# Attention scores of the two smallest query chunks in plain float32, with one head in each of two opposite quarters of the array

## The chip, the cores and the metric

The kernel runs on one core of a Trainium2 chip. The metric is the device time of the whole program in microseconds (us), as the median of several runs. The core has a tensor engine (PE, with its weight loads shown as PEld), VectorE (DVE), ScalarE (ACT), GpSimd (POOL) and SyncE (SP), whose queue issues nearly all of the DMAs here.

## What is computed

Three layers follow one another: causal attention with a bias from a cumulative sum, a dense feed-forward layer, and a layer of eight experts of which each token takes one. Only the first is touched. Cut to what matters:

```python
# q, k, v: (4, 8, 576, 64) float32; s: (4, 8, 576)
scores = (1 / sqrt(64)) * (q @ k.T)
cum = cumsum(maximum(s, 0), axis=-1)
bias = -(cum[:, :, :, None] - cum[:, :, None, :])
scores = where(causal, -1e9, scores + minimum(bias, 0))
attn = exp(scores - scores.max(-1))
attn = attn / (attn.sum(-1) + 1e-9)
x = attn @ v                                  # then to (2304, 512)
x = (h - tanh(h)) @ w_out,  h = x @ w_in
out = expert layer of x, one expert for a token
```

## The kernel before

The attention works on 16 pairs of heads (4 batches with 4 pairs each). `attention_events` makes the work of one pair as a list of events, each with a time in schedule steps; a pair starts every 9 steps, and all events of all pairs are sorted by these times. On PE the instructions stand in exactly this order (`manual_schedule` with `ORD[MA]`, which holds PE alone); on the other engines and on SP's queue a scheduler orders them by its own model, with the time of the event as priority.

For each pair the 576 queries are cut into nine chunks of 64 (`NCH`). Chunk c sees the first 64c + 64 keys. A chunk's scores for both heads stand in one PSUM tile `sc`: head 0 in partitions 0 to 63, head 1 in 64 to 127. They come from one matmul over all 128 rows: the queries stand in `qb` as blocks (rows 0 to 63 and columns 0 to 63 for head 0, rows 64 to 127 and columns 64 to 127 for head 1, zeros between), the keys of both heads one under the other. To keep precision, queries and keys are split in a rounded high part and the rest (`qh`, `ql`, `kh`, `kl`, type float32r), and three products are added (L235 and L236). The split is made per pair by ACT (L192, L200: the high parts) and by POOL (L183, in `low`: the rests; for the first pair by DVE).

The chunks are scored from the largest (c = 8, step 0 of the pair) to the smallest (c = 0, step 8). Chunks 2 and 0 share the PSUM tile of chunks 3 and 1 (`SECOND`): chunk 1 fills columns 0 to 127, chunk 0 columns 128 to 191, and then one mask matmul in bfloat16 adds the causal mask for both (L243). For the other chunks the mask is a matmul of its own (L246). DVE adds the bias and takes the row minimum (L254), ACT takes the exponential (L258). PE then transposes the weights in groups of four blocks of 128 by 128 (`ptr`, L273), DVE and ACT copy them to `PT` (L137), and PE multiplies them with the values (`pv`, L292), plain float32, head 0 into partitions 0 to 63 and head 1 into 64 to 127. On PE one group of transposes stands before chunk 1, one between chunk 1 and chunk 0, and one behind chunk 0's mask.

The denominators `den` are transposed (L318), written to memory (`rden_d`, L325), read back spread over partitions (`rdb`, L343) and multiplied in when `pv` is evacuated (L300). The biases of the scores come from POOL (L211), from rows `cr` that are loaded for each pair (L178). Queries and keys are loaded by L160 as [128, 576] tiles `xq` and `xk`, two buffers each. `pads` (events at step 60.5) clears some records on POOL (L415 to L419) and sends them out through SP (L417, L420). For the last pair the denominators are spread by small plain float32 matmuls instead (L336), written as a loop over chunks and the two heads:

```python
nc.tensor.matmul(
    pt[64 * h:64 * h + 64, 64 * c - o:64 * c - o + 64], k.oh[:, c, :], T["rt"][:, 64 * h:64 * h + 64],
    start=True, stop=True)
```

While the attention runs, ACT and DVE also convert weights of the next layer (L402 to L406). The next layer begins on PE with L597.

Of the kernel before, what the change touches and what calls it, by code (L numbers as in the profile page):

```python
# [8 lines left out]
F32 = mybir.dt.float32  # L9
# [29 lines left out]
def setup_attention(ctx, tc, k, s):  # L39
# [58 lines left out]
    for p in k.P:  # L98
# [10 lines left out]
SECOND = (2, 0)  # L109
# [4 lines left out]
BIAS = 'PPPPPPPPP'  # L114
LO = 'PPP'

AT = {'ni': 14, 'no': 2, 'pad': 60.5, 'const': 42.5, 'wl': 6.2, 'cr': -9.0, 'load': -20.0, 'v': 6.0, 'ks': -9.5, 'qs': -8.5,
# [11 lines left out]
def behind(tc, k, eng, ins):  # L129

    if eng in k.mark:
        tc.add_manual_dep(
            ins.ins, k.mark[eng], mybir.DependencyInfo(mybir.DependencyClass.NoSync, mybir.DependencyReason.DATA), reason="queued behind")
# [6 lines left out]
def attention_events(tc, k, q, kk, v, xT, b, hp, idx):  # L140

    nc = tc.nc
# [3 lines left out]
    T = {}  # L146
    P = k.P[idx % 2]
    qh, ql = k.qb[idx % NQB]

    def at(t):  # L150
        def deco(f):
            ev.append((9 * idx + t, f))
            return f
        return deco

    @at(AT["load"])
    def _():
        for src, nm in ((kk, "xk"), (q, "xq")):
            t = T[nm] = k.e1.tile([128, S], F32, name=nm, tag=nm, bufs=2)
            nc.sync.dma_start(t, src[b, hp])  # L160

    @at(AT["v"])
    def _():
        t = T["vt"] = ld.tile([128, 2, 5, D], F32, name="vt", tag="vt", bufs=2)
        nc.sync.dma_start(t.rearrange("p a c d -> p (a c d)"), v[b, hp])

    @at(AT["cr"] if idx else AT["qs"] + 0.1)
    def _():
# [12 lines left out]
    def low(eng, l, x, h):  # L181
        pool = idx and eng == "P"
        ins = (nc.gpsimd if pool else nc.vector).tensor_tensor(l, x, h.bitcast(F32), ALU.subtract)  # L183
        if pool:
            behind(tc, k, "P", ins)
            k.mark["P"] = ins.ins.name

    @at(AT["ks"])
    def _():
# [4 lines left out]

    @at(AT["qs"])
    def _():
        for h in range(2):
            p, o = slice(64 * h, 64 * h + 64), slice(64 * h, 64 * h + 64)
            x = T["xq"][p].rearrange("p (c i) -> p c i", i=64)
            behind(tc, k, "A", nc.scalar.copy(qh[p, :, o], x))  # L200
            low(LO[1 + h], ql[p, :, o], x, qh[p, :, o])

    def chunk(c, lo=0, hi=None):
        return P[:, PW[c] + lo:PW[c] + (64 * c + 64 if hi is None else hi)]
# [1 line left out]
    def bias(c):  # L206

        w = 64 * c + 64
        ci = k.cumi[:, c, bh // 2:bh // 2 + 1]
        if BIAS[c] == "P" and (idx or c % 2):  # L210
            ins = nc.gpsimd.tensor_scalar(chunk(c), T["cr"][:, 0:w], 1.0, ci, ALU.mult, ALU.add)  # L211
            behind(tc, k, "P", ins)
            k.mark["P"] = ins.ins.name
        else:
            nc.vector.tensor_scalar(chunk(c), T["cr"][:, 0:w], ci, None, ALU.add)


    def score(c):
        if c == NCH - 1:
            T["m"] = wk.tile([128, NCH], F32, name="m", tag="m")  # L220
            T["m2"] = wk.tile([128, 1], F32, name="m2", tag="m2")
            T["den"] = wk.tile([128, NCH], F32, name="den", tag="den")
        w = 64 * c + 64

        if w > 512:
            cuts = [(0, 288, 0), (288, 576, 0)]
        else:
            cuts = [(0, w, 64 * c + 128 if c in SECOND else 0)]
        for lo, hi, o in cuts:
            two = c in SECOND or c - 1 in SECOND  # L230
            if c not in SECOND:
                T["sc"] = ps.tile([128, 512], F32, name="sc", tag="sc")
            sc, n = T["sc"], hi - lo

            for i, (a, x) in enumerate(((qh, "kh"), (qh, "kl"), (ql, "kh"))):  # L235
                nc.tensor.matmul(  # L236
                    sc[:, o:o + n], a[:, c, :], T[x][:, lo:hi], start=(i == 0 and c not in SECOND), stop=(i == 2 and hi < w))
            if c - 1 in SECOND:
                continue
            if c in SECOND:  # L240

                d = sc[:, o - 64:o + n].rearrange("p (a j) -> p a j", j=64)
                nc.tensor.matmul(  # L243
                    d[:, 0::c + 1, :], k.identb, k.maskm.unsqueeze(1).broadcast_to((128, 2, 64)), start=False, stop=True)
            elif hi == w:
                nc.tensor.matmul(sc[:, n - 64:n], k.identb, k.maskm, start=False, stop=True)  # L246
            if c in SECOND:
                least(c + 1, sc, 0, 0, w + 64, 3.0e38)
            least(c, sc, o, lo, hi, 3.0e38 if lo == 0 else T["m2"])

    def least(c, sc, o, lo, hi, start):
        dst = chunk(c, lo, hi)
        m = T["m"][:, c:c + 1] if hi == 64 * c + 64 else T["m2"]
        k.mark["D"] = nc.vector.tensor_tensor_reduce(  # L254
            out=dst, in0=sc[:, o:o + hi - lo], in1=dst, scale=-0.125, scalar=start, op0=ALU.add, op1=ALU.min, accum_out=m).ins.name
# [5 lines left out]
    for n in range(NCH):  # L261
        at(n + AT["bias"] - (4 if idx == 0 and n % 2 else 0))(lambda c=NCH - 1 - n: bias(c))
        at(n)(lambda c=NCH - 1 - n: score(c))
        at(n + AT["exp"] + (0.6 if NCH - 2 - n in SECOND else 0))(lambda c=NCH - 1 - n: expo(c))
# [734 lines left out]
def tile_kernel(ctx, tc, q, kk, v, s, w_in, w_out, w_gate, w_og, w1, w2, out, dbg=None):  # L999
# [7 lines left out]
    with ExitStack() as abctx:  # L1007
# [3 lines left out]
        with ExitStack() as actx:  # L1011
# [14 lines left out]
            for i in range(16):  # L1026
                ev += attention_events(tc, k, q, kk, v, xT, i // 4, i % 4, i)
# [81 lines left out]
```

## Time and profile before

| | us |
|---|---|
| median of 3 runs | 928.68 (928.37 to 930.35) |
| the profiled execution | 928.81 |
| its span in the profile | 927.1 |
| attention, from the start to the first L597 matmul on PE | 197.5 |
| busy over the span: PE, DVE, ACT, POOL | 884.7 (95%), 613.5 (66%), 537.9 (58%), 367.4 (40%) |

The profile lists for each instruction its start and duration on the profiled execution. The ends of matmuls are modelled, and matmuls overlap in the array, so a matmul's price is read from start to start and not from its duration. A row of the timeline merges instructions of the same line and form that follow one another: its first number is the start of the first, its second the time from there to the end of the last, and "x4" their count; with the duration of a single one the start of the last is found. In brackets stand the idle time of the engine before the row and what ended it. The same line can be called "L292 pv<-PT,vt": it writes `pv` and reads `PT` and `vt`; "128*64" are the array's rows and columns that it uses.

### The profile page before, as it was taken

Reading aid. Unit: us, or ns where it says so; the run is one execution under the profiler, and the core shown is the slowest. Engines: PE = TensorE matmul, PEld = TensorE weight load, DVE = VectorE, ACT = ScalarE, POOL = GpSimd, SP = SyncE. Lnnn points to the kernel's source line nnn. Section 1 sums busy time; section 2 is a strip of 40 time slices with the busy share of each in tenths; the row PEclk is TensorE's granted clock in tenths of the full one; section 3 lists DMA queues with packets and bytes.
Section 4 is the critical chain, followed back from the end, with each engine's and each line's share of the span. In section 5 each row is a group of like instructions: output and inputs, shape, how many; then the busy total and the mean of one; then the engine's idle time right before and its main releaser. Section 6 shows DMA issues by size and latency. Waiting matters only on the chain.

```text
span 927.1 us, 16181 instructions
## 1 busy us (share of the span) xinstructions
PE 884.7 (95%) x5808; PEld 757.2 (82%) x5809; DVE 613.5 (66%) x1343; ACT 537.9 (58%) x1092; POOL 367.4 (40%) x396
## 2 busy tenths in 40 slices
PE   7999999988998999999999999999799999999995
PEld 5777787777877778888989898988688888888884
DVE  8988988969888887786565656577435444444420
ACT  6887888856666667465555555565254444444421
POOL 8999788725444432342222232322230220221011
PEclk9999999999999999999999999999999999999998
DMA  6676776562212211000000000422655554565100
GB/s 210 202 209 191 228 211 185 191 234 69 58 57 69 69 46 69 1 24 2 24 1 24 2 23 1 124 105 91 151 209 169 164 179 152 167 191 145 49 25 30
DMA packets 41362, 100.82 MB, mean 109 GB/s; under 512 B 9314, under 2 KB 9446, under 8 KB 41278
## 3 DMA queue, kind: packets, MB, share of 16 engines
q1 hardware_dynamic: 37117, 89.51, 31.4%
q0 software_dynamic: 4160, 10.23, 3.2%
q8 instruction: 47, 0.77, 0.4%
q14 instruction: 38, 0.30, 0.1%
HBM read 84.74 MB, written 15.79 MB: 108 GB/s over the span
## 4 chain that ended last, share of the span: by engine, by line
PE 62%; DVE 14%; issue 9%; ACT 5%; POOL 4%; DMA 4%; SPq 1%; DVEq 0%; POOLq 0%; ACTq 0%
PE h L597 14%; PE x L627 12%; PE y L864 12%; PE hc L840 10%; PE sc L236 4%; PE pv L292 3%; DVE d L609 3%; PE tp L273 3%; DVE t L611 3%; POOL P L211 2%; DVE d L607 2%; DVE wt L405 1%; DVE wt L406 1%; DMA rdb<-rden_d 1%; ACT u L604 1%
## 5 line engine op out<-in xcount | busy, mean ns | idle before, releaser
L597 PE MATMUL h<-x_h,wi 128*128 128x256 f32 x1152 | 221.4, 285 | 3.3 <-DVE t L610 3.3
L614 POOL TENSOR_TENSOR gl<-t,gh 128x512 fp32r<-128x512 f32 x72 | 100.4, 1395 | 259.8 <-ACT gh L613 173.0
L597 PEld LDWEIGHTS h<-x_h,wi 128*128 128x128 f32 x1152 | 184.0, 191 | 11.2 <-PE x L627 6.4
L627 PE MATMUL x<-wo,gh 128*128 128x512 f32 x576 | 180.0, 393 | 0.3 <-POOL wo L545 0.3
L597 PE MATMUL h<-x_l,wi 128*128 128x256 f32 x576 | 162.8, 283 | 0.0
L627 PE MATMUL x<-wo,gl 128*128 128x512 f32 x288 | 114.8, 399 | 8.4 <-POOL gl L614 8.3
L607 DVE TENSOR_TENSOR d<-u,h 128x512 f32<-128x512 f32 x72 | 49.4, 686 | 105.5 <-ACT t L606 105.4
L627 PEld LDWEIGHTS x<-wo,gh 128*128 128x128 f32 x576 | 103.6, 189 | 18.6 <-POOL wo L545 0.7
L597 PEld LDWEIGHTS h<-x_l,wi 128*128 128x128 f32 x576 | 110.2, 191 | 1.3
L236 PE MATMUL sc<-kh,qb 128*128 128x288 f32 (+8 forms) x320 | 100.7, 344 | 0.0
L258 ACT ACTIVATE P<-P,m 128x576 f32<-128x576 f32 (+2 forms) x144 | 81.1, 566 | 22.7 <-DVE m L254 22.1
L613 ACT CAST gh<-t 128x512 fp32r<-128x512 f32 x72 | 44.7, 621 | 83.3 <-DVE t L611 59.8
L827 DVE SCALAR_TENSOR_TENSOR gl<-hc,gh 128x336 fp32r<-128x336 f32 (+2 forms) x66 | 32.8, 497 | 90.5 <-ACT gh L826 84.0
L211 POOL TENSOR_SCALAR P<-cr,cumi 128x448 f32<-128x448 f32 (+4 forms) x139 | 88.1, 650 | 1.9 <-ACT cr L137 0.4
L826 ACT ACTIVATE gh<-hc 128x336 fp32r<-128x336 f32 (+2 forms) x66 | 29.2, 443 | 94.9 <-PE hc L840 83.2
L840 PE MATMUL hc<-xgh,w_h 128*128 128x336 f32 (+1 forms) x256 | 82.1, 321 | 0.0
L762 DVE TENSOR_TENSOR w_l<-w_r,w_h 128x1024 fp32r<-128x1024 f32 (+1 forms) x72 | 79.4, 1112 | 3.3 <-PE h L597 2.7
L840 PE MATMUL hc<-xgh,w_l 128*128 128x336 f32 (+1 forms) x256 | 79.9, 312 | 0.0
L840 PE MATMUL hc<-xgl,w_h 128*128 128x336 f32 (+1 forms) x256 | 79.7, 312 | 0.0
L627 PEld LDWEIGHTS x<-wo,gl 128*128 128x128 f32 x288 | 54.1, 188 | 27.6 <-POOL gl L614 16.3
L864 PE MATMUL y<-w_h,gh 128*128 128x512 f32 (+1 forms) x192 | 76.1, 397 | 0.0
L864 PE MATMUL y<-w_l,gh 128*128 128x512 f32 (+1 forms) x192 | 76.0, 396 | 0.0
(194 smaller groups left out, 1932.0 us busy)
## 6 DMA issues: line engine op xcount, KB each, us to landing
w_r<-in_moe_w_dram SPq DMA_DIRECT2D x64, 512.0 KB, 3.6
f64raw<-in_moe_w_in_dram SPq DMA_DIRECT2D x16, 512.0 KB
f64raw<-in_moe_w_out_dram SPq DMA_DIRECT2D x16, 512.0 KB, 3.5
vt<-in_v_dram SPq DMA_DIRECT2D x16, 320.0 KB, 3.5
xk<-in_k_dram SPq DMA_DIRECT2D x16, 288.0 KB, 3.6
xq<-in_q_dram SPq DMA_DIRECT2D x16, 288.0 KB, 4.6
x_d<-x2s SPq DMA_DIRECT2D x9, 512.0 KB
cr<-cum_d SPq DMA_DIRECT2D x30, 144.0 KB, 3.7
```

What stands on the lines that cost most here:

```text
L211: ins = nc.gpsimd.tensor_scalar(chunk(c), T["cr"][:, 0:w], 1.0, ci, ALU.mult, ALU.add)
L236: nc.tensor.matmul(sc[:, o:o + n], a[:, c, :], T[x][:, lo:hi], start=(i == 0 and c not in SECOND), stop=(i == 2 and hi < w))
L258: k.mark["A"] = nc.scalar.activation(chunk(c), chunk(c), AF.Exp, bias=T["m"][:, c:c + 1], scale=-1.0, accum_out=T["den"][:, c:c + 1]).ins.name
L597: nc.tensor.matmul(ps[:, i, :], a[f][:, c, :], x[:, c, :], start=(n == 0), stop=(n == 11))
L607: nc.vector.tensor_tensor(d, u, ps, ALU.mult)
L613: nc.scalar.copy(gh, t)
L614: k.mark["P"] = nc.gpsimd.tensor_tensor(gl, t, gh.bitcast(F32), ALU.subtract).ins.name
L627: nc.tensor.matmul(st["x2", g][t], a[:, i, 128 * t:128 * t + 128], w[f], start=(f == 0 and n == 0), stop=(f == 15 and n == 2),)
L762: pin(tc, "1D"[e > 0], nc.vector.tensor_tensor(l[:, a:z], r[:, a:z], h[:, a:z].bitcast(F32), ALU.subtract))
L827: nc.vector.scalar_tensor_tensor(l, ps, 0.0, h.bitcast(F32), ALU.max, ALU.subtract)
L840: nc.tensor.matmul(ps[:, 0:w], a[:, c, fo:fo + 128], x, start=(n == 0), stop=(n == 11))
L864: nc.tensor.matmul(st["y", e, c][0:n, :], a[:, o:o + n], w, start=(f == 0 and i == 0), stop=(f == 7 and i == 2),)
```

## The change

Chunks 1 and 0 no longer take the split queries and keys. Their first 128 queries and keys are loaded a second time, by two small DMAs per pair into tiles of their own (`xk0`, `xq0`, [128, 128] float32, two buffers, at step -5 of the pair), and for each head one plain float32 matmul over 64 rows and 64 columns of the array takes the place of the three split ones: head 0 from partitions 0 to 63 into partitions 0 to 63, head 1 from 64 to 127 into 64 to 127. The splits of the queries leave out chunks 0 and 1 (448 columns in the place of 576); those of the keys stay whole. The mask, the order of events on PE and all else are as before.

```diff
+    @at(AT["f"])                      # AT['f'] = -5.0
+    def _():
+        for s, nm in ((kk, "xk0"), (q, "xq0")):
+            t = T[nm] = k.e1.tile([128, 128], F32, name=nm, tag=nm, bufs=2)
+            nc.sync.dma_start(t, s[b, hp, :, 0:128])
...
-            x = T["xq"][p].rearrange("p (c i) -> p c i", i=64)
-            behind(tc, k, "A", nc.scalar.copy(qh[p, :, o], x))
-            low(LO[1 + h], ql[p, :, o], x, qh[p, :, o])
+            x = T["xq"][p].rearrange("p (c i) -> p c i", i=64)[:, 2:, :]
+            behind(tc, k, "A", nc.scalar.copy(qh[p, 2:, o], x))
+            low(LO[1 + h], ql[p, 2:, o], x, qh[p, 2:, o])
...
-            for i, (a, x) in enumerate(((qh, "kh"), (qh, "kl"), (ql, "kh"))):
-                nc.tensor.matmul(
-                    sc[:, o:o + n], a[:, c, :], T[x][:, lo:hi], start=(i == 0 and c not in SECOND), stop=(i == 2 and hi < w))
+            if c < 2:
+                for h in range(2):
+                    p = slice(64 * h, 64 * h + 64)
+                    nc.tensor.matmul(
+                        sc[p, o:o + n], T["xq0"][p, 64 * c:64 * c + 64], T["xk0"][p, 0:w], start=(c not in SECOND), stop=False)
+            else:
+                for i, (a, x) in enumerate(((qh, "kh"), (qh, "kl"), (ql, "kh"))):
+                    nc.tensor.matmul(
+                        sc[:, o:o + n], a[:, c, :], T[x][:, lo:hi], start=(i == 0 and c not in SECOND), stop=(i == 2 and hi < w))
```

## Rows read from the trace of the kernel before

**Rows 1.** PE's timeline at the attention's end

```profile
197.53 0.39 PE L597 MATMUL h<-x_h,wi 128*128 128x256 f32 x1
```

**Rows 2.** Busy time by stretch: PE, PEld, DVE, ACT, POOL, granted clock, DMA share, GB/s

```profile
48.00:92.00 44.00, 42.87 (x354) 34.47 (x352) 37.42 (x126) 36.85 (x104) 41.65 (x61) 1.00 0.67 194
```

**Rows 3.** PE's timeline: the pv matmuls of chunks 4 to 8, once per pair

```profile
30.86 0.49 PE L292 MATMUL pv<-PT,vt 128*64 128x320 f32 x2
...
41.88 0.49 PE L292 MATMUL pv<-PT,vt 128*64 128x320 f32 x2
...
99.07 2.28 PE L292 MATMUL pv<-PT,vt 128*64 128x320 f32 x20
...
110.09 2.28 PE L292 MATMUL pv<-PT,vt 128*64 128x320 f32 x20
```

**Rows 4.** PE's timeline where it stood still; one wait (us, times, longest)

```profile
23.80 0.27 PE L318 MATMUL tp<-ident,den 128*9 128x128 f32 x1 [1.29 <-DVE den L313]
...
92.41 0.87 PE L292 MATMUL pv<-PT,vt 128*64 128x256 f32 x8 [1.54 <-DVE xT L300]
...
148.16 0.62 PE L292 MATMUL pv<-PT,vt 128*64 128x256 f32 x3 [0.20 <-DVE xT L300]
...
187.68 0.88 PE L273 MATMUL tp<-ident,P 128*128 128x128 f32 x3 [0.94 <-ACT PT L137]
...
DVE xT L300 <- DMA rdb<-rden_d: 4.1, 5, 2.2
```

**Rows 5.** PE's timeline around chunks 1 and 0 of one pair

```profile
105.99 0.61 PE L273 MATMUL tp<-ident,P 128*128 128x128 f32 x4
...
106.72 0.62 PE L273 MATMUL tp<-ident,P 128*128 128x128 f32 x4
107.10 0.28 PE L236 MATMUL sc<-kh,qb 128*128 128x64 f32 x1
...
107.44 0.23 PE L243 MATMUL sc<-maskm,identb 128*128 128x128 bf16 x1
107.51 0.61 PE L273 MATMUL tp<-ident,P 128*128 128x128 f32 x4
```

**Rows 6.** Plain float32: L292's records (duration ns), then PE's timeline of L336

```profile
L292 PE MATMUL pv<-PT,vt x448: 219/380/484, 30.9 to 197.3; 128*64 128x320 f32 x64, 128*64 128x256 f32 x22, 128*64 128x128 f32 x22, 128*64 128x192 f32 x21
...
191.92 1.26 PE L336 MATMUL sc<-rt,oh 9*64 9x64 f32 x36 [0.34 <-ACT rt L320]
...
191.92 0.33 PE L336 MATMUL sc<-rt,oh 9*64 9x64 f32 x4 [0.34 <-ACT rt L320]
```

**Rows 7.** PE's timeline where it goes into and out of pv

```profile
188.29 0.38 PE L273 MATMUL tp<-ident,P 128*128 128x128 f32 x2
188.60 1.02 PE L292 MATMUL pv<-PT,vt 128*64 128x320 f32 x5
...
104.11 0.60 PE L292 MATMUL pv<-PT,vt 128*64 128x256 f32 x6
104.64 0.33 PE L273 MATMUL tp<-ident,P 128*128 128x128 f32 x1
...
190.60 0.28 PE L292 MATMUL pv<-PT,vt 128*64 128x64 f32 x4
190.81 0.44 PE L273 MATMUL tp<-ident,P 128*128 128x128 f32 x2
```

**Rows 8.** Instructions of L183 and L160: duration ns min/median/max, first and last start

```profile
L183 POOL TENSOR_TENSOR qb<-xq,qb x30: 1403/1421/1866, 14.5 to 169.8; 64x576 fp32r<-64x576 f32 x30
...
L160 SPq DMA_DIRECT2D xq<-in_q_dram x6: 327/328/328, 91.7 to 149.0; - x6
```

**Rows 9.** Timelines of SP's queue and of POOL around the pads

```profile
77.79 0.48 SPq L393 DMA_DIRECT2D f64raw<-in_moe_w_in_dram  x1
84.77 0.34 SPq L417 DMA_DIRECT2D recs_d<-pad  x1
...
84.52 0.23 POOL L416 MEMSET pad<- 128x152 int32 x1
```

More of the change, by code (lines that the diff above doesn't have):

```diff
@@ L115 @@
 LO = 'PPP'
-AT = {'ni': 14, 'no': 2, 'pad': 60.5, 'const': 42.5, 'wl': 6.2, 'cr': -9.0, 'load': -20.0, 'v': 6.0, 'ks': -9.5, 'qs': -8.5,
+AT = {'ni': 14, 'no': 2, 'pad': 60.5, 'const': 42.5, 'wl': 6.2, 'cr': -9.0, 'load': -20.0, 'f': -5.0, 'v': 6.0, 'ks': -9.5, 'qs': -8.5,
       'bias': -4.0, 'exp': 0.8, 'n0': 9.2, 'n1': 11.55,
```

## The prediction

> **What bounds the kernel now.** The page's shares come first: the tensor engine (PE) is busy 95% of the span. But that is a mean over stages, and the change touches one stage alone, the attention, which ends with the first L597 matmul at 197.53 us [rows 1]. There I read the busy time by stretch: in the 44 us from 48 to 92 PE is busy 42.87 and GpSimd (POOL) 41.65, the granted clock is 1.00, the higher of the two levels (2.4 GHz) [rows 2]. Busy time can't tell which of the two sets the pace, so I took one mark that comes once per head pair, the first `pv` matmul of chunks 4 to 8: 30.86 and 41.88, later 99.07 and 110.09 [rows 3]; ten of the fourteen steps between such marks are like these, 11.01 to 11.12 us. Where PE isn't idle between two marks and the step is always the same, PE's own order of matmuls sets the pace. The longer steps hold stalls: 1.54 us of idle before the `pv` at 92.41, while DVE's evacuation of the one before waited for the `rdb` load; 0.20 at 148.16; 0.94 at 187.68, for a PT copy; and at the start 1.29 before L318 [rows 4]. L597's row shows no idle time before it [rows 1], and so I carry what the attention gains or loses to the end one to one.
>
> **What is removed on PE.** Chunks 1 and 0 are short scores between groups of four transposes. Group to group it takes 0.73 us with chunk 1 between (105.99 to 106.72) and 0.79 with chunk 0 and its mask (106.72 to 107.51) [rows 5]. Four transposes alone stand 0.11 apart (four end 0.61 after the first starts, and one takes 0.27: 0.34 for three steps), so 0.44 of each is theirs. Chunk 1 costs 0.29 us and chunk 0 with mask 0.35. Chunk 0's three take 0.34 to the mask (107.10 to 107.44), 0.11 each, though they have 64 columns, half of chunk 1's: their price is not in the columns. From the mask to the next transpose are 0.07 [rows 5].
>
> **What is added on PE.** A plain float32 matmul stands twice in the trace: `pv` has 448 records, 28 per pair, for 14 calls [rows 6]. So each chunk becomes two passes for each head. The nearest rows are L336, written alike (two heads, 64 columns of output each, 64 columns moved): its records come in twos, 36 of them in 1.26 us with 0.22 for one, so 18 twos in 1.04 us, 0.06 apart, the first step 0.11 (192.03 after 191.92) [rows 6]. The two heads run side by side: 64 columns take 0.05 to 0.06, and 128 about 0.11 (below). That alone would make a chunk cheap: 0.22 for chunk 1, 0.12 for chunk 0.
>
> But the array is then divided otherwise than for the transposes and the mask around it, and the rows show what that costs. *Into a 64-column form:* from the last transpose at 188.40 (188.29 and 0.38 for two, 0.27 one) to `pv` at 188.60 are 0.20, instead of 0.11 [rows 7]. *First pass:* 0.11 instead of 0.06 in L336, so 0.05 [rows 6]. *Out of it:* the last two `pv` of 64 columns stand at 190.66 (four in 0.28, one 0.22) and the transpose behind them at 190.81: 0.15 for 0.05 of columns, so 0.10. *After it:* the next transpose stands at 190.98 (0.44 for two, 0.27 one), 0.17 instead of 0.11 [rows 7]. Together 0.3 us for one block between transposes. (From 104.11 to 104.64 a pass of 256 columns, two of 128 and the way out take 0.53: less 0.10 that is 0.11 for 128 [rows 7].)
>
> Chunk 1 anew: 0.20 in, 0.16 to the second pass, 0.20 out, less the 0.11 that the last transpose has anyway, 0.05 after: 0.50, against 0.29: +0.21. Chunk 0: 0.20, 0.11, 0.15, then the bf16 mask and 0.07 as now, less 0.11: 0.42; its way out goes to the mask and not to a transpose, for which no row stands, so between nothing and 0.1 more; I take 0.05, the transposes' after-cost: 0.47 against 0.35, +0.12. **+0.33 us per pair, 16 pairs, +5.3 us.** From below, were the changeovers free, chunk 1 is 0.07 cheaper (0.22 for 0.29) and chunk 0 0.16 (0.12 and 0.07 for 0.35): -0.23 per pair. From above, were the heads not side by side, +0.32 more: +0.65. I take +0.33, since both the side by side and the changeover have rows with 64 columns of output on each half.
>
> The Trainium skill, TensorEngine Tiling (Array Packing), Theoretical Speedup, gives up to 2x for each dimension of at most 64, which would have this change gain. The same page, Tiling Modes, Key Properties, says that changing the tiling mode drains the engine; by that rule something is paid back at each of the four changeovers, as the rows above show, and the page states no price for it. By the first rule alone the sum would be under zero, by both together of either sign.
>
> **What lies beside other work.** ScalarE's two casts and POOL's two L183 subtractions go from 576 to 448 columns; the latter from 1.42 us to about 1.10 by the columns, 0.64 less of POOL for each pair, the casts by less [rows 8]. Neither ends a step of 11.01, so I cost them at nothing, with one exception below. The two added loads have 64 KB each; an L160 issue holds SP's sequencer 0.33 us, so 0.7 us per pair [rows 8]. Their slots were read two pairs earlier, so they wait for nothing, and they are asked for 12 schedule steps (of 9 in 11.01 us, so 14.7 us) ahead of chunk 1. What they are put ahead of on SP is `rden_d` and `rdb`; DVE waited for `rdb` in 5 places, 4.1 us together [rows 4]. Behind DVE's wait stand the copies and reductions that free PSUM for PE. One `pv` ends at 101.35 (99.07 and 2.28) and the next has its second pass at 104.11 [rows 3, 7], so a late `rdb` has some 2.5 us before PE notices; I leave this at 0; from above 0.7 us in four pairs, 2.8; below nothing there is no gain, because a load can't make `rdb` earlier.
>
> **What stalls give back.** A PE that comes later waits less where another engine set the time. At 92 us PE is late by 7.5 times 0.33, 2.5 us, and the 1.54 of waiting there came from elsewhere: SP stood from 78.27 to 84.77 for POOL's `pad`, with `rden_d` and `rdb` queued behind it, and POOL came to that only at 84.52 [rows 9]. POOL is lighter too, by 0.64 us per pair. So 1.5 is taken up, and the 0.2 at 148.16 and pair 0's 0.3 in the wait before L318 likewise [rows 4]. The stop at 187.68 hangs on the chain `den`, `rden_d`, `rdb`, which starts from PE itself and so moves with it; only what PE does meanwhile counts, one and a half pairs, 0.5. Sum: 1.5 + 0.2 + 0.3 + 0.5 = 2.5. **5.3 - 2.5 = +2.8 us.** The profiled execution took 928.81 us (its span is 927.1, and 1.7 lie around it), 0.13 above the median of 928.68, so the forecast against the median is 931.5.
>
> **The rivals.** *The quarters make the changeover cheap (faster).* Both heads have rows and columns of their own, so weights might be loaded without emptying the array. Then -0.23 per pair, -3.7, and POOL's lighter queue still removes the 1.5 at 92 us: 923.5. It decides where the changeovers cost under 0.23 of the 0.56 us per pair that I count. Against it: `pv` and L336 pay for them [rows 6, 7]. For it: neither of them divides the rows in halves.
>
> *The heads don't run side by side.* In L336 and `pv` both heads use the same rows of the array; here one has the upper and one the lower half, and both write one bank of PSUM. If they wait for each other it is +0.32 more per pair, 5.1 us: 936.6. The same page of the Trainium skill, Restrictions and Gotchas, Gotcha 1: PSUM Pressure, says that different row tiles can't access the same PSUM bank at once; by that rule this is the case that comes. No run here shows it; against it stands only that the heads write different partitions of the bank.
>
> *No difference.* The cost after a changeover (0.05, twice) stays away: +0.23 per pair, 3.7. And POOL's first biases, queued behind its first subtractions, come 0.6 earlier into the wait before L318: 3.7 - 2.5 - 0.6 = +0.6, 929.3.
>
> *SP is late.* The 2.8 us of above come on top: 934.3.
>
> **How the numbers follow.** Forecast 0.45, heads one after the other 0.12, SP late 0.10, no difference 0.18, faster 0.15. A measurement of this kernel can tell about 0.2%, 1.9 us, from none; +2.8 is near that, so 0.07 of the forecast's chance falls under it: faster 0.15, same 0.25, slower 0.60. The range takes in the late SP, the serial heads, no difference and the milder part of the faster case: 926.0 to 937.0; outside remain the full gain and what goes beyond the serial heads, under 0.2 together.
>
> **What would show it.** In the new trace: the `pv` mark every 11.3 to 11.4 us; the four transposes before chunk 1 some 0.94 from the next four, those before chunk 0 some 0.91; score records of 64 columns in twos less than 0.02 apart (serial heads: each alone, 0.05 or 0.10 apart); the wait at 92 us gone; L183 at 1.1 us. I am wrong if the step falls under 11.0 us, or if the 0.20 into the quarters reads 0.11.

## The result, and the profile after

The changed kernel takes 933.94 us (median of 19 runs; before, run beside it, 930.22): the ratio on record is 1.0057, with an interval of 1.0035 to 1.0078 (the quotient of the two medians is 1.0040; every ratio below is the one on record, with its interval in brackets). It is slower, by about 0.6%; the forecast was 931.5 against 928.68, a ratio of 1.0030. Where a kernel here has several runs, before too, they spread over 8 to 13 us (most of the longer ones have a mean granted clock of 0.983 to 0.987 in place of 0.990 to 0.995), so the intervals are 0.2 to 0.45% to either side, and what is smaller is read from the traces.

The page of after, its head and the busy time of PE and POOL (share of the span, instructions):

```profile
span 932.3 us, 16294 instructions
PE 890.8 (96%) x5840; PEld 754.0 (81%) x5841; DVE 611.8 (66%) x1343; ACT 534.4 (57%) x1092; POOL 355.3 (38%) x396
```

PE is 6.1 us busier than before and POOL 12.1 us less. The span is 5.2 us longer. PE's timeline of after (start, time to the end of the last, engine, line, form, count), with the lines that answer to [rows 1] and [rows 3]:

```profile
32.08 2.28 PE L305 MATMUL pv<-PT,vt 128*64 128x320 f32 x20
...
56.29 2.28 PE L305 MATMUL pv<-PT,vt 128*64 128x320 f32 x20
67.62 2.28 PE L305 MATMUL pv<-PT,vt 128*64 128x320 f32 x20
...
203.94 0.39 PE L610 MATMUL h<-x_h,wi 128*128 128x256 f32 x1
```

An undisturbed step between two marks is 11.33 us (56.29 to 67.62), where it was 11.01 to 11.02: +0.31 for each pair. The attention ends at 203.94 instead of 197.53, +6.4 us. The rest of the span takes 728.4 us (before 729.6); in the other traces of this study, which are alike there, it takes 727.6 to 730.1, but for 735.7 in the second trace of after, which is one of those longer runs, so that there is nothing to explain in it.

PE's timeline around chunks 1 and 0, which answers to [rows 5]:

```profile
191.48 0.60 PE L286 MATMUL tp<-ident,P 128*128 128x128 f32 x4
192.02 0.44 PE L245 MATMUL sc<-xk,xq 64*64 64x128 f32 x4
192.39 0.66 PE L286 MATMUL tp<-ident,P 128*128 128x128 f32 x4
192.97 0.33 PE L245 MATMUL sc<-xk,xq 64*64 64x64 f32 x4
193.24 0.23 PE L256 MATMUL sc<-maskm,identb 128*128 128x128 bf16 x1
193.30 0.72 PE L286 MATMUL tp<-ident,P 128*128 128x128 f32 x5
```

From group to group it is 0.91 with chunk 1 between (0.73 before) and 0.91 with chunk 0 and its mask (0.79): +0.30 together. Four records of 64 columns take 0.33 with 0.22 for the last one alone, so 0.11 for all four starts: the two heads' records start 0.007 apart, and the second pass 0.10 later. The heads run side by side.

After's window of 48 to 92 us, with the columns of [rows 2], and the line of the shorter subtraction, which answers to L183 in [rows 8] (duration in ns, least, median, most):

```profile
48.00:92.00 44.00, 43.27 (x356) 33.08 (x356) 36.77 (x130) 36.66 (x106) 37.00 (x59) 1.00 0.69 208
```
```profile
L189 POOL TENSOR_TENSOR qb<-xq,qb x30: 1136/1142/1152, 14.5 to 176.9; 64x448 fp32r<-64x448 f32 x30
```

POOL has 37.00 us in place of 41.65; the subtraction takes 1.14 in place of 1.42. So much went as forecast. What didn't is in PE's stops. The timeline of after where it stood still in front of `pv`, with the length of the stop and what ended it:

```profile
38.24 0.87 PE L305 MATMUL pv<-PT,vt 128*64 128x256 f32 x8 [1.33 <-DVE xT L313]
...
73.19 0.87 PE L305 MATMUL pv<-PT,vt 128*64 128x256 f32 x8 [0.73 <-DVE xT L313]
...
107.62 0.65 PE L305 MATMUL pv<-PT,vt 128*64 128x256 f32 x4 [0.22 <-DVE xT L313]
...
119.43 0.83 PE L305 MATMUL pv<-PT,vt 128*64 128x256 f32 x7 [0.25 <-DVE xT L313]
...
142.97 0.87 PE L305 MATMUL pv<-PT,vt 128*64 128x256 f32 x8 [0.54 <-DVE xT L313]
...
166.38 0.87 PE L305 MATMUL pv<-PT,vt 128*64 128x256 f32 x8 [0.26 <-DVE xT L313]
```

The stop of 1.54 at 92 us is gone [rows 4], and these six have come, with a seventh of 0.07 at 154.59. Counted from start to start, beyond the 0.13 that the way into this `pv` always takes, and without the last pair's, which is 0.68 in both, PE waits 3.9 us in front of `pv`, and 1.9 before. The start of the same `pv` mark in the two kernels shows where the 6.4 us arise (worked out from the marks of both timelines, pair by pair):

```
mark          1    2    3    4    5    6    7    8    9    10   11   12   13   14   15   16   first h
after-before  1.22 3.08 3.39 3.71 4.89 5.20 3.49 4.25 5.05 5.47 6.56 6.47 7.25 6.87 6.30 6.42 6.41
```

It grows by 0.31 where nothing waits (marks 2 to 4, 5 to 6), jumps by more where after waits for `rdb` (marks 2, 5, 8, 9, 11, 13), and falls where before did (mark 7 is the stop at 92 us, marks 14 and 15 those at 176 and 187). Of the 1.22 at the first mark, 1.02 were there before the first new matmul ran (the row of the transposes behind the first wait for ACT stands at 17.43, and at 16.41 before); a second trace of the same kernel has its first mark at 31.11, and over all traces of this study it lies between 30.86 and 32.68, two traces of one kernel 1.0 and 1.5 apart. So that first us isn't shown to be the change's, and kernels are better compared from mark 1 to mark 15: 157.7 us in before, 162.8 in after, +5.1.

### The profile page after: what moved, and what is told of

Same layout as the page of the kernel before. It is cut to its first block, busy times and chain, and to the rows that moved or that the text cites. A ratio compares the mean times of both kernels' runs of the same rounds, so it can differ in the third digit from the quotient of the medians.

```text
span 932.3 us, 16294 instructions
## 1 busy us (share of the span) xinstructions
PE 890.8 (96%) x5840; PEld 754.0 (81%) x5841; DVE 611.8 (66%) x1343; ACT 534.4 (57%) x1092; POOL 355.3 (38%) x396
## 4 chain that ended last, share of the span: by engine, by line
PE 64%; DVE 13%; issue 9%; ACT 5%; DMA 4%; POOL 3%; SPq 0%; DVEq 0%; POOLq 0%; ACTq 0%
PE h L610 14%; PE x L640 12%; PE y L877 12%; PE hc L853 10%; PE sc L249 4%; PE pv L305 4%; PE tp L286 4%; DVE d L622 3%; DVE t L624 3%; DVE d L620 2%; DMA rdb<-rden_d 1%; DMA rden_d<-rt 1%; DVE wt L418 1%; DVE wt L419 1%; ACT u L617 1%
## 5 line engine op out<-in xcount | busy, mean ns | idle before, releaser
L610 PE MATMUL h<-x_l,wi 128*128 128x256 f32 x576 | 162.8, 283 | 0.0
L217 POOL TENSOR_SCALAR P<-cr,cumi 128x448 f32<-128x448 f32 (+4 forms) x139 | 84.6, 625 | 1.9 <-ACT cr L137 0.4
L249 PE MATMUL sc<-kh,qb 128*128 128x288 f32 (+6 forms) x256 | 85.1, 362 | 0.0
```

What stands on the lines that cost most here:

```text
L249: nc.tensor.matmul(sc[:, o:o + n], a[:, c, :], T[x][:, lo:hi], start=(i == 0 and c not in SECOND), stop=(i == 2 and hi < w))
L610: nc.tensor.matmul(ps[:, i, :], a[f][:, c, :], x[:, c, :], start=(n == 0), stop=(n == 11))
```

## Where the wait for rdb comes from

The chain that ended last, taken over 30 to 200 us (share of the stretch by line, then pieces with start and length), first of before, then of after:

```profile
by line: PE sc L236 19.9%; PE pv L292 18.2%; PE tp L273 14.0%; POOL P L211 9.2%; DMA rdb<-rden_d 6.5%; issue 5.2%; POOL qb L183 5.0%; DMA rden_d<-rt 2.8%; ACT P L258 2.2%; DVE P L254 1.5%; PE h L597 1.5%; DVE xT L300 1.3%; POOL kl L183 1.3%
...
162.59 2.23 DMA rden_d<-rt
165.34 3.93 DMA rdb<-rden_d
```
```profile
by line: PE sc L249 23.7%; PE tp L286 21.1%; PE pv L305 20.4%; DMA rdb<-rden_d 8.2%; DMA rden_d<-rt 7.7%; PE sc L245 4.1%; issue 2.1%; ACT P L271 2.0%; PE sc L256 1.5%; POOL qb L189 1.3%; PE sc L259 1.3%; DVE xT L313 1.2%; ACT PT L137 0.9%;
...
108.81 5.36 DMA rden_d<-rt
114.68 3.93 DMA rdb<-rden_d
```

POOL, with 14% of before's chain in two lines, has nearly left it. The two DMAs of the denominators have gone from 9.3% to 15.9%. The reading `rdb` lands after 3.93 us in both; the writing `rden_d` takes 5.36 us in after and 2.23 in before. What stands ahead of it is read on SP's queue (start, length of the issue), of after and then of before, with the two writes of the chain above among the lines:

```profile
107.44 0.33 SPq L160 DMA_DIRECT2D xq<-in_q_dram  x1
107.86 0.38 SPq L1055 DMA_DIRECT2D wi_f<-wf  x1
108.29 0.42 SPq L406 DMA_DIRECT2D f64raw<-in_moe_w_in_dram  x1
108.81 0.37 SPq L338 DMA_DIRECT2D rden_d<-rt  x1
...
114.18 1.55 SPq L356 DMA_DIRECT2D rdb<-rden_d  x2
```
```profile
112.23 0.33 SPq L1042 DMA_DIRECT2D wi_f<-wf  x1
112.61 0.42 SPq L393 DMA_DIRECT2D f64raw<-in_moe_w_in_dram  x1
115.51 0.33 SPq L160 DMA_DIRECT2D xq<-in_q_dram  x1
115.93 1.31 SPq L325 DMA_DIRECT2D rden_d<-rt  x1
...
119.07 1.09 SPq L343 DMA_DIRECT2D rdb<-rden_d  x2
...
157.56 0.38 SPq L393 DMA_DIRECT2D f64raw<-in_moe_w_in_dram  x1
...
162.59 0.46 SPq L325 DMA_DIRECT2D rden_d<-rt  x1
```

The order on SP has changed, though the change wrote nothing there but two loads. Before, the 512 KB of `f64raw` went out while `xq` stood waiting for POOL, and `rden_d` 3.3 us behind it. Now `xq` goes first, and `f64raw` 0.5 us ahead of `rden_d`. The chip can't show why the scheduler chose so; that this order is what makes `rdb` late is the theory that the runs below test. The two writes shown are far apart in their landing; the median over the pairs is 3.1 us in before and 4.4 in after. Over all writes that SP issues in the twelve traces of this study in which it issues them, the 54 that stand within 0.7 us of an `f64raw` load (from `in_moe_w_in` or `in_moe_w_out`) landed after a median of 4.5 us (3.3 to 6.1), and the 43 that stand 6 us or more behind one after 2.5 (1.4 to 4.2). The Trainium skill, DMA: Bandwidth & Descriptors, Queues, rings and completion order, says that each DMA engine takes descriptors of one row in the order of its ring; by that rule a small write issued just behind a bulk load waits for its turn, and the 5.36 against 2.23 us agree. That it is the order in the ring is not shown: where ACT issues the write instead (two of the runs below), one 0.4 us and one 0.45 us behind such a load still landed after 4.6 and 4.9 us.

As a measure I took, pair by pair, the time from the transposing of `den` on PE to the landing of the second `rdb`: a median of 10.3 us in before and 12.1 in after. Of the 1.8 us, 0.2 lie ahead of the write's issue (2.6 and 2.9 us after the transposing) and 1.3 in its landing. The seven stops in after stand in the pairs with 12.1 to 12.7 us (in the same pairs before has 8.3 to 13.0), and of the pairs under 12 us none has one; DVE's evacuation that PE waits for begins 0.12 us after the second `rdb` has landed in six of the seven, and 0.47 after it in the last.

## Experiments on the price of the array's changeover

The theory: on PE the time is lost in going from the full array into 64-column form and back, twice per pair, and not in the products. Rivals: dividing the rows has a price of its own; or the heads disturb each other in PSUM.

**Columns halved, rows whole.** The queries of each head stand in a block with zeros, and each head's matmul uses all 128 rows and 64 columns. (The same edit needs three small loads instead of two, and two tiles that POOL clears once; that part is left out below, here and for the whole array.)

```diff
-                    nc.tensor.matmul(
-                        sc[p, o:o + n], T["xq0"][p, 64 * c:64 * c + 64], T["xk0"][p, 0:w], start=(c not in SECOND), stop=False)
+                    nc.tensor.matmul(sc[p, o:o + n], T["xq0"][:, c, p], T["xk0"][:, 0:w], start=(c not in SECOND), stop=False)
```

> As whole_array, but each chunk in two calls, one for each head: all 128 rows (with the zeros of the block tile), 64 columns of the array each. It has the changeover into a 64-column form without dividing the rows. Theory: entering and leaving the 64-column form is what costs, whatever the rows; then the step is 11.33 us as in the changed kernel, and the records of the two heads stand 0.007 us apart. Rival: the division of the rows has a price of its own; then the step lies under 11.2 us.

PE's timeline of it, chunks 1 and 0:

```profile
117.87 0.44 PE L251 MATMUL sc<-xk,q 128*64 128x128 f32 x4
118.24 0.66 PE L291 MATMUL tp<-ident,P 128*128 128x128 f32 x4
118.82 0.34 PE L251 MATMUL sc<-xk,q 128*64 128x64 f32 x4
119.09 0.23 PE L261 MATMUL sc<-maskm,identb 128*128 128x128 bf16 x1
```

The step is 11.33, as in after, and the starts stand as in after (0.37 from chunk 1 to the transposes, 0.27 from chunk 0 to the mask). Dividing the rows has no price of its own, nor does the use of other rows make the changeover cheap. Its one run took 927.88 us; the attention ended at 198.51, since PE waited only 0.2 us in front of `pv`.

**The whole array.** Queries in blocks with zeros for both heads, one plain float32 matmul per chunk over 128 rows and 128 columns; no changeover is left.

```diff
-                for h in range(2):
-                    p = slice(64 * h, 64 * h + 64)
-                    nc.tensor.matmul(
-                        sc[p, o:o + n], T["xq0"][p, 64 * c:64 * c + 64], T["xk0"][p, 0:w], start=(c not in SECOND), stop=False)
+                nc.tensor.matmul(sc[:, o:o + n], T["xq0"][:, c, :], T["xk0"][:, 0:w], start=(c not in SECOND), stop=False)
```

> The changed kernel with the two chunks' plain float32 scores in the whole array: the raw queries of both heads are loaded into a tile with zeros between (blocks as in the split form), so that one call serves both heads and no changeover is left; three small loads per pair. Theory: the price of the change on PE is the changeover, not plain float32. Then two passes of 0.11 us each replace three split ones of 0.11, the mark of pv comes every 10.8 us (11.01 less 2 times 0.11), and the time lies 2 to 5 us under the changed kernel's at least, with a ratio to the kernel before of 0.996 to 1.001 after waits for rdb. Rival: plain float32 itself is dear; then the step stays above 11.2 us.

```profile
115.70 0.60 PE L289 MATMUL tp<-ident,P 128*128 128x128 f32 x4
116.14 0.39 PE L249 MATMUL sc<-xk,q 128*128 128x128 f32 x2
116.36 0.60 PE L289 MATMUL tp<-ident,P 128*128 128x128 f32 x4
116.80 0.33 PE L249 MATMUL sc<-xk,q 128*128 128x64 f32 x2
116.97 0.22 PE L259 MATMUL sc<-maskm,identb 128*128 128x128 bf16 x1
117.02 0.61 PE L289 MATMUL tp<-ident,P 128*128 128x128 f32 x4
```

That is its timeline of PE. Both intervals are 0.66, and the step is 10.83: the same products are 0.5 us per pair cheaper than in quarters and 0.18 cheaper than the split ones. The time was 925.41 us, a ratio of 0.9968 (0.9923 to 1.0012). A second set of runs of the same kernel gave 927.71 and 0.9988 (0.9959 to 1.0017):

> The kernel with plain float32 in the whole array, again, beside the changed kernel. Theory (the changeover is the price): step 10.83 us, ratio to the kernel before 0.994 to 0.999, 7 to 9 us under the changed kernel. Rival (the first measurement was the chip's own spread): a ratio of 1.000 or more.

Its step is again 10.83, but its trace has 1.9 us of waits in front of `pv`, where the first had none. PE's gain is certain; that the whole is faster than before is not shown, as both intervals reach over 1. That it is faster than the quarters is: the ten runs of this second set and ten of after on the same chip (934.04, below) have medians 6.3 us apart, and of the 100 pairs of one run each after's is the longer in 95.

**One changeover instead of two.** Chunk 1 is scored right ahead of chunk 0, so that the two stand in one block.

```diff
-        at(n)(lambda c=NCH - 1 - n: score(c))
+        at(n if n != 7 else 7.95)(lambda c=NCH - 1 - n: score(c))
```

> The changed kernel with chunk 1 scored right ahead of chunk 0, without the group of transposes between them: one way into the quarters and one out of them per pair instead of two. Theory: one changeover costs 0.10 in, 0.05 first pass, 0.10 out and 0.05 after, so the step falls from 11.33 to 11.03 to 11.08 us where PE doesn't wait; the waits for rdb stay (SP's order is that of the changed kernel). Rival (the price is in the plain float32 passes): the step stays at 11.3.

PE's timeline of it:

```profile
115.76 1.04 PE L286 MATMUL tp<-ident,P 128*128 128x128 f32 x8
116.73 0.55 PE L245 MATMUL sc<-xk,xq 64*64 64x128 f32 x8
117.21 0.23 PE L256 MATMUL sc<-maskm,identb 128*128 128x128 bf16 x1
117.28 0.60 PE L286 MATMUL tp<-ident,P 128*128 128x128 f32 x4
```

From the first group of transposes to the one behind the mask are 1.52 us, as in before (105.99 to 107.51, [rows 5]), and 1.82 in after; the step is 11.04. So with two changeovers it is 11.33, with one 11.04, with none 10.83: the second of two costs 0.29 us, and the one that is left, whose way out goes to the mask, 0.21. The one run took 927.50 us, with 1.8 us of waits in front of `pv`.

## Experiments on the wait for rdb

**The two loads alone.** Before, with the two small loads added; nothing reads them.

```diff
+    @at(AT["f"])                      # AT['f'] = -5.0
+    def _():
+        for s, nm in ((kk, "xk0"), (q, "xq0")):
+            t = T[nm] = k.e1.tile([128, 128], F32, name=nm, tag=nm, bufs=2)
+            nc.sync.dma_start(t, s[b, hp, :, 0:128])
```

> The kernel before, with the two small loads per pair added and nothing that reads them; scores, splits and order of PE as before. If the changeovers on PE are what sets the longer step, the mark of pv comes every 11.01 us here as in the kernel before. What the loads cost by themselves is then the difference in waits: 0 to 4 us (ratio 1.000 to 1.004). If the loads were the main loss of the change, the ratio would be near 1.0055 here.

928.65 us, a ratio of 0.9992 (0.9955 to 1.0029); the step is 11.01, the attention ends at 197.29, and the waits in front of `pv` are 1.5 us. But the run tests less than it was meant to: with nothing that reads the tiles the scheduler sent all 32 loads by 90.6 us, up to five ahead of one `rden_d`, where after sends two per pair until 176 us. Up to there the loads and their issue time cost nothing that can be seen (`f64raw` stands up to 1 us ahead of `rden_d` in five of these pairs, and goes out ahead of the wait of `xq`, as in before, in most of the later ones). That the two loads in their places aren't the loss either is seen in the next run and in that of the later bulk load, which keep them and lose most of the waits; with them the rival of a late SP falls in the form in which it was put.

**The splits left whole.** After, with the splits over all 576 columns again.

```diff
-            x = T["xq"][p].rearrange("p (c i) -> p c i", i=64)[:, 2:, :]
+            x = T["xq"][p].rearrange("p (c i) -> p c i", i=64)
```
(and `qh[p, 2:, o]`, `ql[p, 2:, o]` as `qh[p, :, o]`, `ql[p, :, o]`)

> The changed kernel with the splits of the queries made over all 576 columns as before, so that POOL and ScalarE have the work that they had; scores and loads as in the changed kernel. Theory: POOL doesn't set the pace, so the step stays 11.33; the shorter splits have their effect through SP's order alone (here rden_d stands ahead of the xq load instead of behind it), so the waits of pv fall under 2 us. Rival (POOL's 0.64 us per pair count by themselves): the step is longer than 11.33 or stalls on POOL come back at 90 us.

One run, 931.26 us. The step stays 11.33 with POOL's subtraction back at 1.42 us: POOL's saving doesn't set PE's pace. On SP's queue `xq` now goes behind `rden_d`, which is issued 0.6 us after `den`'s transposing (2.9 in after), and the time to `rdb` falls to 8.7 us. So the shorter splits act through SP's order; the one run's time says nothing here. That they do it because they free the buffer of `xq` earlier is argued, not shown.

**The denominators' write off SP's queue.** After, with `rden_d` issued by ACT, and the same edit in before.

```diff
-        nc.sync.dma_start(
+        nc.scalar.dma_start(
             k.rden_d[bh:bh + 2].rearrange("h (c i) -> c h i", i=64), rt.rearrange("c (h i) -> c h i", h=2))
```

> The changed kernel, with one edit: the write of the denominators (rden_d) is issued from ScalarE's queue, where the tile that it sends was just copied, instead of standing in SP's queue behind the loads of f64raw, wi_f and xq. Theory: the changed kernel loses twice, 0.31 us per pair on PE at the changeovers and about 3.9 us in waits of pv for rdb, because rden_d stands behind bulk loads. Then the mark of pv still comes every 11.33 us, the time from the den transpose to the landing of the second rdb falls from about 12.5 us to 10 or less, the idle time of PE before pv falls from 3.3 us to under 1, and the time lies 3 to 4 us under that of the changed kernel (ratio to the kernel before 1.000 to 1.003). Rival: the waits come from PE's longer step or from DVE's order, not from this queue; then the waits and the ratio of about 1.0055 stay.

> The kernel before, with the same single edit (rden_d issued from ScalarE's queue). Theory: the kernel before has less of this wait, 1.6 us at 92 us (behind the pads) and 0.3 at 148 us; it should gain 1.5 to 3 us (ratio 0.997 to 0.9985), less than the changed kernel gains by the same edit. Rival (queue without influence): 1.000.

In after the waits in front of `pv` fall from 3.9 to 0.85 us and the attention ends at 200.75, but the time doesn't show it: 937.27 us, a ratio of 1.0057 (1.0018 to 1.0097). In before the ratio is 0.9996 (0.9962 to 1.0029), the waits stay at 1.8. The waits followed the queue; neither time came as expected. The trace of the former is of the fastest of its ten runs (930.11), so that it may not stand for the other nine; in time the pair does not bear the theory out, and why stays open.

**The bulk load later.** `f64raw` is asked for three schedule steps later, in after and in before. The first of the two runs stood beside a second set of runs of after.

```diff
-      'n2': 13.0, 'w0': 5.4, 'wt': (0, 1.2, 2.2, 3.2, 4.2), 'ws': 6.0, 'wd': 9, 'wr': 8}
+      'n2': 13.0, 'w0': 5.4, 'wt': (0, 1.2, 2.2, 3.2, 4.2), 'ws': 6.0, 'wd': 9, 'wr': 5.0}
```

> The changed kernel with one number changed: the 512 KB load of f64raw is asked for 3 steps later, so that in SP's queue it stands behind rdb and no longer right ahead of rden_d; PE's order is the same. Theory: the changed kernel's waits of pv (3.9 us) come from rden_d landing late (about 5.4 us after its issue, 3.3 in the kernel before) behind that load. Then rden_d lands in about 3.5 us, the waits fall by 2 us or more, the step stays 11.33, and the time falls by 1 to 3 us under the changed kernel's. Rival (the waits have another cause, DVE's order or PE's longer step): no change of the waits.

> The changed kernel itself, so that the others of this group have it on the same chip. Both theories: ratio 1.004 to 1.007, the mark of pv every 11.33 us where PE doesn't wait, waits of pv for its evacuation 3 to 4 us beyond the usual.

After as it is: 934.04 us, a ratio of 1.0029 (0.9995 to 1.0062), step 11.33, waits 3.7 us, 11.3 us to `rdb`. With the bulk load later: 930.24, a ratio of 1.0012 (0.9979 to 1.0045), the same step, waits 0.2. Each against before, the two intervals overlap; against each other, ten runs on the same chip each, the medians are 3.8 us apart, and of the 100 pairs of one run each after's is the longer in 81. PE's timeline of the latter, and its chain over 30 to 200 us:

```profile
65.61 2.28 PE L305 MATMUL pv<-PT,vt 128*64 128x320 f32 x20
76.94 2.28 PE L305 MATMUL pv<-PT,vt 128*64 128x320 f32 x20
...
198.81 0.38 PE L610 MATMUL h<-x_h,wi 128*128 128x256 f32 x1
```
```profile
by line: PE sc L249 31.1%; PE pv L305 26.5%; PE tp L286 24.5%; PE sc L245 4.8%; PE sc L256 1.8%; PE sc L259 1.7%; DMA rdb<-rden_d 1.5%; DMA rden_d<-rt 1.4%; issue 1.0%; PE tp L331 1.0%; DVE P L267 0.8%; PE sc L349 0.7%; PE h L610 0.7%; DVE 
```

The denominators' DMAs are down from 15.9% to 2.9% of the chain, and the attention ends 5.1 us earlier than in after, 1.3 us later than in before. On this queue `f64raw` stands behind `rdb`, and `rden_d` lands after a median of 2.7 us.

> The kernel before, with the load of f64raw asked for 3 steps later. Theory: it helps where rden_d is late; the kernel before has that in few places (1.9 us of waits of pv, 1.6 of them behind the pads), so it gains 0 to 2 us (ratio 0.998 to 1.000), less than the changed kernel does by the same edit (3.7 us between the medians). Rival: the edit helps any kernel by 3 us or more; then bulk_load_later says nothing on the change.

In before the same edit made things worse: 932.48 us, a ratio of 1.0052 (1.0021 to 1.0083), which wasn't expected. The step is still 11.01. Its waits:

```profile
DVE xT L300 <- DMA rdb<-rden_d: 8.7, 7, 2.7
PE pv L292 <- DVE xT L300: 3.7, 4, 1.6
```

(total us, times, longest). The attention ends at 202.50. In this order `f64raw` goes between `rden_d` and `rdb`, and `rden_d` itself is issued 4.4 us after the transposing of `den` in place of 2.6. So with PE's work as it was, and waits for `rdb` like those of after, the ratio is near that of the whole change. Of the 5.0 us in its trace 1.4 were there at the first mark; the 3.6 behind it are more than the 2.1 us of waits in front of `pv` that came on top, and what the later load does to the work that needs it was not separated. The edit is no remedy by itself, since what counts is the order that comes out.

> Plain float32 in the whole array, and the load of f64raw asked for 3 steps later as in bulk_load_later. Theory: both losses of the change are gone, the changeovers (step 10.83 us) and the late rden_d (waits of pv under 0.5 us); the attention ends 3 us or more before that of the kernel before, ratio 0.993 to 0.998. Rival (other engines are the bound by then): the step shows more stalls on the transposes, ratio 0.998 to 1.000.

With the whole array the later bulk load brought nothing: 928.00 us, a ratio of 0.9993 (0.9958 to 1.0029), step 10.83, waits 2.2 us. This too was expected otherwise. Put side by side, worked out from the traces (us; the median over the pairs of the time from `den`'s transposing to the second `rdb`, the waits in front of `pv`, the undisturbed step, the way from mark 1 to mark 15, the end of the attention):

```
kernel                    to rdb   waits   step    1 to 15   end
before                      10.3    1.9    11.01     157.7   197.5
loads_alone                  9.9    1.5    11.01     157.2   197.3
before_rden_own_queue       10.4    1.8    11.01     158.3   199.2
before_bulk_load_later      11.3    4.0    11.01     161.3   202.5
after                       12.1    3.9    11.33     162.8   203.9
changed_again               11.3    3.7    11.33     162.3   203.3
rden_own_queue              10.6    0.9    11.33     159.1   200.8
bulk_load_later             10.2    0.2    11.33     158.1   198.8
splits_whole                 8.7    0.8    11.33     158.8   200.0
column_halves                8.7    0.2    11.33     158.4   198.5
chunks_adjacent             10.9    1.8    11.04     158.1   198.1
whole_array                  9.1    0.0    10.83     153.7   195.1
whole_array_again            9.4    1.9    10.83     156.2   198.6
whole_array_later           10.3    2.2    10.83     156.1   196.6
```

The three traces over 11 us, with some 4 us of waits, are the three that are longest from mark 1 to mark 15; under that the order is not strict, and one kernel's executions differ by 2 us in their waits and by 2.4 from mark to mark. In the timed ratios `rden_own_queue` is as slow as after (1.0057), which its trace does not show. That a shorter step leaves less time for `rdb`, so that a kernel that is quicker on PE waits more at the same delay, fits the last four rows and is argued, not shown.

## Why the prediction was right, and which step was off

**PE's price, +0.33 per pair, was right: +0.31.** Into the 64-column form 0.20, the first pass of 128 columns 0.15, the way out to the transposes 0.20, the next transpose 0.165 behind the first in place of 0.11: each as taken from `pv` and L336. The intervals read 0.91 and 0.91 (0.94 and 0.91 were forecast, with the after-cost put into the first; it stands in the second). What was not there is the 0.05 taken for chunk 0's way out to the mask: from the mask to the next transpose are 0.066, no more than before (0.072). Over 16 pairs that is 5.0 in place of 5.3.

**The heads side by side: right.** Their records start 0.007 us apart, in one bank of PSUM and from different rows of the array, and take no longer than those of the run with whole rows (0.37 and 0.27 in both). The Trainium skill's rule that different row tiles can't access one bank at once (TensorEngine Tiling (Array Packing), Restrictions and Gotchas, Gotcha 1) would have them wait for each other; no such wait is seen here, where they write different partitions of it; what becomes of two row tiles on the same partitions wasn't tried. The rule of the same page of the Trainium skill, Tiling Modes, Key Properties, that changing the mode drains the engine, agrees with the 0.21 and 0.29 us of the two changeovers.

**The cheap changeover: wrong.** It would have needed the 0.20 to read 0.11. The run with whole rows shows the same 0.20, so that the halves of the rows neither help nor hurt.

**What stalls give back, 2.5: the terms came, and more, but the sum was mis-sized.** The stop at 92 us went (1.54; the step that holds it is 13.03, 2.0 over the others, as 0.4 more are lost at the transposes behind it), that at 148 us fell from 0.20 to 0.07 (154.59 in after), and L318's wait from 1.29 to 1.03. At the end more came back than the 0.5 that was taken: the difference falls by 0.95 over marks 13 to 15, though PE's own work adds to it there. What failed is that no new stop was counted: with what is left of the one at 148 us, seven in front of `pv`, for `rdb`, make the 3.9 us. The text left a late `rdb` at 0, with 2.8 as the bound from above, and had it as a rival of chance 0.10, SP late, at 934.3. In effect that is the case that came, near the measured ratio; in mechanism it is not, as `rden_d` is issued only 0.2 us later, and the waits are gone with the two loads still in place (bulk load later, 0.2 us). The slots of the small loads were not always free, as the text had it: between 20 and 185 us SP waited in ten places for PE ahead of one, 5.1 us together. The slack of 2.5 us before PE notices was read from one pair, correctly, and it was used up: the time to `rdb` grew by 1.8 us as a median, and by 2.4 to 4.3 in four of the seven pairs with a stop, because the whole queue was ordered anew, the bulk load directly ahead of `rden_d`. I had looked at what is put ahead of `rden_d` only among the instructions that the diff adds, and not at those that the scheduler would move around them.

**Sum.** From mark 1 to mark 15 PE's +0.31 per pair makes 4.4 us. Without the late `rdb` the traces have +0.4 (bulk load later) and +0.7 (columns halved) against before, so the stalls give back near 4 us, and not 2.5; with it they have +5.1 and +4.5 (the two traces of after), so the late `rdb` costs some 4 to 5 us, and not 0. The forecast had 2.8 in all. In the timed ratios it is 1.0057 and 1.0029 with the late `rdb` against 1.0012 without; their intervals overlap, and the direct comparison on one chip (934.04 against 930.24) is what tells the two apart. So the sign and the price on PE were right for the reasons given. The middle of the forecast is about half of what the ratio says (0.0057 of 930, 5.3 us), and that it came so near is in part luck: too little was counted on either side.

**What stays open.** Why the scheduler orders SP's queue as it does in each kernel; how much of the waits belongs to one execution and not to the kernel (no wait and 1.9 us in two traces of the same whole-array kernel); why the run with the write on ACT's queue is no faster in time, though its trace waits less; and whether the whole array is faster than before: from mark 1 to mark 15 its three traces are 1.5 to 4.0 us shorter, and none of its three intervals settles it.

## What to carry to other kernels

A small matmul between large ones is priced by the rows around it: going from the full array into a 64-column form and back costs time here (0.5 us for the two changeovers of a pair), and the smaller form saved no pass against zeros in blocks over the whole array, where one call serves both heads too. So the blocks, or putting the small pieces side by side, cost PE less than the packing. Where a scheduler orders a queue, an edit that shortens one engine's work moves everything on the queue: ask which small, urgent transfer stands behind which bulk load, and read its landing time, not only who issues what. A stop that vanishes says nothing of the sum until the new stops are counted.

## What the runs showed of the hardware

One changeover into 64 columns and back costs 0.29 us between transposes and 0.21 with the way out to the mask (steps of 11.33, 11.04 and 10.83), with 64 or with 128 rows in use alike (11.33 in both). Within the block the products are cheap in either form: chunk 0 takes 0.17 us from its first pass to the mask over the whole array, and 0.27 in quarters, of which the way out is a good part. For chunk 1 the entry is 0.20 from the last transpose in place of 0.11, the first pass 0.15 in place of 0.11, the way out 0.20 in place of 0.11, and the next transpose 0.165 behind the first in place of 0.11. A small write that is issued 0.5 us behind a load of 512 KB on the same queue landed after 5.36 us, and one issued 5.0 us behind such a load (157.56 and 162.59 in before) after 2.23; over all of them the medians are 4.5 within 0.7 us and 2.5 from 6 us on.
